# Beacon attention and low-rank mixer on one core: the first pair's masks ahead of casts, and three turns by DMA kept apart from the loads

## The chip, the cores and the metric

The kernel runs on one core of one Trainium2 chip. The core has a matmul engine (TensorE, "PE" in the profile; its weight loads are "PEld"), a vector engine (VectorE, "DVE"), a scalar engine (ScalarE, "ACT"), a general engine (GpSimd, "POOL") and a sync engine (SyncE, "SP"). Each works through its own instructions in order and waits on semaphores of the others. In this kernel POOL issues nearly all loads, and SP issues the first loads, all transposes by DMA and all stores. The metric is device time in microseconds (us), the median of several runs; lower is better.

## The reference

Batch 8, 8 heads, 576 tokens, 16 beacon tokens, head size 64. The attention's output, heads side by side, is the input of a mixer with a low-rank mixing over tokens and an MLP over channels.

```python
k_all = concat([beacon_k, k], axis=2);  v_all = concat([beacon_v, v], axis=2)
scores = (q @ k_all.T) / sqrt(64)
scores[:, 16:] is masked causally; the 16 beacons are seen by all
a = softmax(scores);  x = (a @ v_all), heads merged: (8, 576, 512)
h = (x.transpose(0, 2, 1) @ U) @ V          # rank 32, over the 576 tokens
u = x + h.transpose(0, 2, 1)
out = u + relu(u @ w_ch1) @ w_ch2           # 512 -> 2048 -> 512
```

## The kernel before

**Pairs.** Heads are treated two at a time: 8 batches of 4 pairs, pairs 0 to 31, so batch 4 is pairs 16 to 19. For one pair the work is as follows. Its q and its k are *grouped*: a copy puts the main 512 tokens of the two heads into a pair tile `pr` (`regroup`, L245 to L247). Then q and k are *transposed*, so that the head size lies on the partitions. For early pairs TensorE does that (`qkT_units`, L249; `tps`). For the others a DMA on SP does it (`turn_pair`, L274 to L280, `raw<-pr`), and a copy from `raw` puts the tokens in order (`order_units`, L282). The tokens that are left over, and the beacons, are turned for all pairs of a batch at once, ahead of the batch's first turn (`turn_heads`, L266, `qT<-hd`, `kT<-hd`). The scores come in two visits of TensorE (`visit`, L304, `sps`), each followed by four exponentials on ACT (L317) into one of four tiles `expt`. Masking is a minimum with a constant on DVE, after the exponentials (`mask_head`, L296: L298 and L300, twice for a pair). Then TensorE multiplies with v (`av_unit`, L331, `po`); a column of ones in v gives the sum, and DVE multiplies with its reciprocal into `xb` (L343, L344).

**Mixing and MLP.** When a batch's four pairs are done, `mix_units` (L359) gives u. From batch 3 on the mixing reads the attention's output turned by DMA (`turn_x`, L352, `xt<-xb`); `mlp_units` (L416) turns u back for the last sum (`ut<-uT`, L425). A block of the MLP is 512 rows: 16 units that compute `gps` (L435, with an eviction by ACT or DVE, L439 and L441) and 16 that compute `cps` (L452, L465). These units wait in a queue.

**Order by hand.** The order on each engine is the order of the words of `SCRIPT` (L687), which `step` (L634) carries out one by one; each engine gets its own instructions in that order, with no scheduler behind it. A number n takes n units from the MLP's queue. `Gk16` with an engine's letter in between, as in `GkA16`, groups k of pair 16 on ACT (V: DVE, G: POOL); `TqV17` is the copy, or the transposes and their copies, that leaves q of pair 17 ready; `R16` issues pair 16's turn on SP, with the batch's head turns if it is the first; `Sa16` and `Sb16` are the two visits of scores with their exponentials (`:2` puts two dummy matmuls ahead, which keep TensorE at work, and `I1` is one such dummy alone); `M16` masks; `A16.0` and `A16.1` multiply with v; `X3.0` to `X3.2` mix batch 3; `x12` turns a part of it; `k5`, `q5`, `v4`, `b5` issue the loads of batch 5's k and q, of batch 4's v and of batch 5's beacon keys on POOL; `Z16` is a copy of one element of pair 16's turned tile on POOL, which makes POOL wait until the turn has landed. In the kernel before, no `Z` stands in the script.

**Buffers.** Pair tiles and `raw` tiles have three buffers each, the load tiles two, `expt` is four tiles (two pairs), and v has two tiles, for even and odd batches. All PSUM tiles come from one pool of eight banks.

The places that the change touches are two: the first microseconds, in which pairs 0 to 3 are cast, scored and masked (their q and k come as 32-bit numbers and are cast while they are grouped), and the stretch in which batch 3 is computed and batch 4's first pairs are turned. There, in the kernel before, the script has: turn 15, then the loads `v4`, then (behind pair 16's grouping on ACT) turn 16; turn 17, then the loads `k5` and `q5`; turn 18 further on.

Of the kernel before, what the change touches and what calls it, by code (L numbers as in the profile page):

```python
# [27 lines left out]
def kernel(  # L28
# [605 lines left out]
    def step(t):  # L634
# [51 lines left out]

    SCRIPT = """  # L687
        v0A u GqA0 I8 GqG1 b1 GkV0 I2 GkG2 HqA0 TqA0 s B 1 v0B HkV0 TkV0 Sa0:3 GkV1 I3 1 TqV1 Sb0 1 TkV1 GqV2
        q1A Sb1 I1 GkV3 M0 GqV3 TkA2 1 w10 cG Sa1:2 TqV2 k1A A0.1 TqV3 M1 TkV3 A0.0 Sb2 Sa2:1 A1.1 A1.0 M2 w11
        q1B Sa3:1 w13 A2.0 GqV5 1 GkG5 Sb3 A2.1 w12 M3 TqA5 eA GqA4 GkA4 I2 A3.0 A3.1 X0.0 X0.1 X0.2 v1A TqA4  # L690
        w20 TkV5 k1B TkA4 w21 3 v1B 1 GqV6 Sb5 1 GqA7 Sa4 1 q2 2 Sb4 2 M4 4 A4.0 Sa5:0 2 GkA6 GkV7 M5 1 TqV6 1
        A5.1 TkA6 b3 A5.0 k2 1 A4.1 TkA7 Sa6:0 1 Sb6 TqV7 GqV8 2 GqV9 Sa7 2 M6 Sb7 b2 1 v2 A6.1 GkV9 GkV8 M7 1
        TqV8 2 GkV10 1 A6.0 GqA10 TqA10 q3 1 A7.1 A7.0 2 X1.0 X1.1 X1.2 TkA10 TqV9 TkV9 1 TkA8 1 Sa9 Sa8 3 Sb8
        1 k3 GqA11 1 v3 Sb9 M8 2 A8.1 A8.0 1 GkV12 1 GqV12 Sa10 1 M9 GkV11 R12 Sb10 1 M10 1 TkV11 1 A10.0
        TqA11 4 GkA13 A9.1 A9.0 Sa11 1 TkV12 GqV15 Sb11 1 k4 A10.1 2 GkA14 GqV13 1 TqA12 b5 Sa12 1 GqA14 M11
        R13 R14 3 GkA15 Sb12 1 A11.0 1 TkV13 M12 A11.1 q4 b4 TqA13 Sa13 R15 A12.0 TkA14 TqV14 1 TqV15 1 GkA16
        GqA16 1 R16 2 Sb13 v4 1 A12.1 M13 X2.0 2 Sb14 GkA17 A13.0 X2.1 TkV15 X2.2 A13.1 Sa14 GqA17 R17 Sb15 k5
        q5 GqA18 1 M14 1 Sa15 x12 3 TkV16 A14.1 TqA16 1 A14.0 k6 4 M15 GkA18 x13 1 R18 TkA17 1 TqV17 Sb16 2
        Sa16 A15.1 GkA19 M16 2 A15.0 TqA18 2 GqA19 x14 GkV20 x15 1 GkA21 1 R19 Sa17 1 A16.0 Sb17 2 GqV20 A16.1
        1 M17 TkA18 Sb18 X3.0 2 X3.1 1 Sa18 A17.0 1 GqA21 M18 1 X3.2 1 TkA19 R20 1 R21 1 GkV22 b6 1 TqA19  # L700
        A18.0 A18.1 v5 1 A17.1 Sa19 4 x18 1 Sb19 TqV20 TkV20 2 M19 GqA22 1 x16 R22 Sb20 A19.1 q6 Sa20 3 M20 1
        TkA21 x17 1 A19.0 1 TqA21 1 A20.0 TqV22 v6 1 GkV23 GqA23 1 x19 R23 Sa21 TkV22 X4.0 1 k7 1 Sb21 1 M21 1
        X4.1 1 A20.1 Sa22 1 A21.0 1 GkV25 GqV24 1 TqA23 GkV24 1 b7 R24 1 TkV23 Sb22 1 q7 A21.1 x20 X4.2 1
        GqA26 M22 GqV25 4 Sa23 x21 A22.0 TkA24 1 Sb23 R25 1 M23 2 A22.1 1 TqA24 A23.1 GkA26 1 R26 Sa24 2 A23.0
        2 Sb24 x22 2 TkA25 TqA25 v7 5 GqV27 1 M24 GkV27 Sa25 2 x23 TkV26 1 A24.0 R27 1 Sb25 TqV26 M25 X5.0
        A24.1 GqV28 2 Sb26 1 GkA28 R28 A25.0 2 x24 Sa26 TqV27 1 X5.1 4 X5.2 1 GkV30 1 TkA27 M26 1 TkV28 A25.1
        GkV29 Sa27 GqV29 2 Sb27 1 A26.0 x25 1 R29 1 M27 A26.1 TqV28 GqA30 1 R30 A27.1 GkV31 2 Sa28 A27.0 1 x26
        1 TqV29 Sb28 2 M28 2 GqV31 TqA30 1 TkA29 TkA30 Sa29 1 X6.0 R31 Sb29 A28.1 x27 A28.0 4 TkV31 2 TqV31 1
        M29 1 Sa30 1 A29.0 2 x28 X6.1 2 Sb30 A29.1 X6.2 4 x29 Sa31 M30 10 Sb31 A30.0 A30.1 2 x30 M31 4 A31.0
        A31.1 2 X7.0 4 x31 1 X7.1 3 X7.2 2  # L710
    """

    with tc.manual_schedule(engines={ENG.PE, ENG.Activation, ENG.DVE, ENG.SP, ENG.Pool}):
# [118 lines left out]
```

## Time and profile before

| | |
|---|---|
| median of 3 runs | 359.29 us (359.05 to 359.36) |
| the profiled execution | 361.73 us, its span 360.1 us |
| TensorE busy | 347.2 us, 96% of the span |
| ACT, DVE, POOL busy | 205.2, 189.9, 84.0 us |
| data moved by DMA | 43.57 MB |

The page gives busy time by engine, the busy tenths in 40 slices, the DMA queues, the chain of work that ended last, the costliest groups, and the DMA issues with the time from issue to landing. In the order of time, a row has its start, its length, the engine, the line, the operation, what it writes and reads, how many instructions are merged in it, and in brackets the engine's idle time before it with the work that ended that wait. A row in which several instructions are merged can hold small gaps.

### The profile page before, as it was taken

Reading aid. Unit: us, or ns where it says so; the run is one execution under the profiler, and the core shown is the slowest. Engines: PE = TensorE matmul, PEld = TensorE weight load, DVE = VectorE, ACT = ScalarE, POOL = GpSimd, SP = SyncE. Lnnn points to the kernel's source line nnn. Section 1 sums busy time; section 2 is a strip of 40 time slices with the busy share of each in tenths; the row PEclk is TensorE's granted clock in tenths of the full one; section 3 lists DMA queues with packets and bytes.
Section 4 is the critical chain, followed back from the end, with each engine's and each line's share of the span. In section 5 each row is a group of like instructions: output and inputs, shape, how many; then the busy total and the mean of one; then the engine's idle time right before and its main releaser. Section 6 shows DMA issues by size and latency. Waiting matters only on the chain.

```text
span 360.1 us, 7694 instructions
## 1 busy us (share of the span) xinstructions
PE 347.2 (96%) x3022; PEld 177.2 (49%) x3022; DVE 189.9 (53%) x530; ACT 205.2 (57%) x432; POOL 84.0 (23%) x123
## 2 busy tenths in 40 slices
PE   7789999999999989999999999999999999999995
PEld 3455478844545435454444444454544544444444
DVE  3775355546649454574767427675554447313311
ACT  4885867399579868658653963678335302401300
POOL 7966648601308005400630050000000000000000
PEclk9989999999999999999999999999999999999998
DMA  9999999992959999996899694563333123013112
GB/s 191 174 172 187 183 191 164 202 160 40 164 127 129 117 162 111 175 223 106 94 163 194 139 107 107 111 116 61 88 100 66 20 76 103 16 58 90 31 48 76
DMA packets 134396, 43.57 MB, mean 121 GB/s; under 512 B 106545, under 2 KB 130353, under 8 KB 134353
## 3 DMA queue, kind: packets, MB, share of 16 engines
q0 software_dynamic: 69008, 17.54, 51.8%
q1 hardware_dynamic: 64752, 25.14, 34.9%
q8 instruction: 25, 0.41, 0.5%
q10 hardware_dynamic: 592, 0.34, 0.3%
q14 instruction: 19, 0.15, 0.1%
HBM read 37.63 MB, written 9.44 MB: 131 GB/s over the span
## 4 chain that ended last, share of the span: by engine, by line
PE 86%; DMA 6%; DVE 2%; ACT 2%; SPq 1%; issue 1%
PE cps L452 35%; PE gps L435 32%; PE po L335 8%; PE sps L311 7%; DMA raw<-pr 4%; DMA sth<-in_q_dram 2%; ACT expt L317 1%; DMA stm<-in_q_dram 1%; PE tps L257 1%; PE ups L394 1%; PE ups L401 1%; PE qtp L375 1%; SPq L190 1%; DVE xb L344 1%; SPq L184 1%
## 5 line engine op out<-in xcount | busy, mean ns | idle before, releaser
L317 ACT ACTIVATE expt<-sps 128x496 f16<-128x496 f32 (+2 forms) x256 | 111.6, 544 | 43.2 <-PE sps L311 39.2
L452 PE MATMUL cps<-w,gT 128*128 128x512 f16 (+1 forms) x656 | 134.2, 353 | 0.0
L435 PE MATMUL gps<-uT,w 128*128 128x512 f16 x576 | 132.7, 379 | 1.1 <-DVE xb L344 1.1
L439 ACT ACTIVATE gT<-gps 128x512 f16<-128x512 f32 x86 | 52.2, 625 | 70.4 <-PE gps L435 70.2
L452 PEld LDWEIGHTS <-gT 128*128 128x128 f16 x656 | 60.5, 98 | 57.5 <-issue 4.4
L435 PEld LDWEIGHTS <-w 128*128 128x128 f16 x576 | 53.0, 98 | 65.1 <-issue 3.5
L441 DVE TENSOR_SCALAR gT<-gps 128x512 f16<-128x512 f32 x58 | 40.0, 690 | 49.5 <-PE gps L435 48.6
L465 DVE TENSOR_TENSOR ob<-cps,ut 128x512 f32<-128x512 f32 (+1 forms) x33 | 22.2, 674 | 47.0 <-PE cps L452 46.6
L335 PEld LDWEIGHTS <-expt 128*128 128x128 f16 (+1 forms) x960 | 36.0, 99 | 14.5 <-DVE expt L298 4.0
L197 POOL DMA_DIRECT2D vs<-in_v_dram x50 | 40.0, 811 | 7.2 <-DMA st<-in_k_dram 4.0
L335 PE MATMUL po<-vs,expt 128*128 128x65 f16 (+1 forms) x960 | 39.2, 195 | 2.3 <-ACT expt L317 1.4
L311 PE MATMUL sps<-qT,kT 64*128 64x80 f16 (+4 forms) x384 | 35.7, 282 | 2.1 <-ACT expt L317 1.2
L344 DVE TENSOR_TENSOR xb<-po,rec 128x320 f16<-128x320 f32 x64 | 31.5, 492 | 2.2
L298 DVE TENSOR_TENSOR expt<-expt,bigmask 128x512 f16<-128x512 f16 x64 | 26.7, 418 | 9.2 <-ACT expt L317 9.2
L343 DVE RECIPROCAL rec<-po 128x5 f32<-128x5 f32 x64 | 12.0, 188 | 28.0 <-PE po L335 27.2
L311 PEld LDWEIGHTS <-kT 64*128 64x128 f16 x384 | 12.5, 94 | 24.4 <-issue 16.4
L187 POOL DMA_DIRECT2D vs<-in_beacon_v_dram x10 | 5.4, 540 | 68.1 <-PE po L335 68.0
L408 DVE TENSOR_TENSOR uT<-ups,xt 128x240 f16<-128x240 f32 (+3 forms) x40 | 15.6, 450 | 7.2 <-PE ups L401 7.2
L518 ACT ACTIVATE pr<-st 128x512 f16<-128x512 f16 x26 | 16.8, 658 | 0.8 <-DMA st<-in_k_dram 0.8
L190 POOL DMA_DIRECT2D st<-in_k_dram x8 | 6.8, 856 | 40.7 <-ACT gT L439 22.9
L518 ACT ACTIVATE qT<-raw 128x512 f16<-128x512 f16 x10 | 11.1, 1105 | 5.3 <-DMA raw<-pr 5.3
L300 DVE TENSOR_TENSOR expt<-expt,mask 80x80 f16<-80x80 f16 x64 | 12.2, 191 | 0.0
(78 smaller groups left out, 170.7 us busy)
## 6 DMA issues: line engine op xcount, KB each, us to landing
out_dram<-ob SPq DMA_DIRECT2D x31, 256.0 KB, 2.2
st<-in_q_dram POOLq DMA_DIRECT2D x6, 512.0 KB, 9.8
st<-in_k_dram POOLq DMA_DIRECT2D x6, 512.0 KB, 8.4
vs<-in_v_dram POOLq DMA_DIRECT2D x18, 128.0 KB, 6.7
w<-in_moe_w_ch_dram POOLq DMA_DIRECT2D x4, 512.0 KB, 8.8
w<-in_moe_w_ch_dram POOLq DMA_DIRECT2D x2, 1024.0 KB, 12.1
out_dram<-ob SPq DMA_DIRECT2D x10, 128.0 KB, 5.7
stm<-in_k_dram SPq DMA_DIRECT2D x4, 256.0 KB, 4.6
```

The lines of the kernel that those rows point to most:

```text
L197: nc.gpsimd.dma_start(out=dst[a : a + nq[j], j, :, :], in_=src[hs, ds(q0[j], nq[j]), :].rearrange("h p d -> p h d"))
L298: nc.vector.tensor_tensor(out=e4, in0=e4, in1=bigmask, op=ALU.min)
L311: nc.tensor.matmul(ps[g, i][:, ds(o, w)], kT[hp, c, ds(P * ch, P)], qT[hp, c, ds(qa, w)], start=True, stop=True,)
L317: nc.scalar.activation(out=ex[i][:, ds(PAD + SLOT * g, gw[g])], in_=ps[g, i][:, 0 : gw[g]], func=AF.Exp, scale=scale)
L335: nc.tensor.matmul(po[:, j, :], ex[0 : nk[c], ds(blk[(c, j)], P)], vs[0 : nk[c], ds(c * H * E + h * E, E)], start=(c == 0), stop=(c == j),)
L344: nc.vector.tensor_tensor(out=xb[:, h // 2, :, ds(D * (h % 2), D)], in0=po[:, :, 0:D], in1=r.broadcast_to([P, NT, D]), op=ALU.mult)
L435: nc.tensor.matmul(g[:, 0:n], w1[:, cc, ts(dc, P)], uT[:, cc, ds(ring(t0), n)], start=(cc == 0), stop=(cc == NCC - 1))
L439: nc.scalar.activation(out=gT["t"][:, dc, 0:n], in_=g[:, 0:n], func=AF.Relu)
L441: nc.vector.tensor_scalar_max(out=gT["t"][:, dc, 0:n], in0=g[:, 0:n], scalar1=0.0)
L452: nc.tensor.matmul(ps[:m, :], gT["t"][:, dc, ds(P * i, m)], w2[:, dc, ds(cs, w)], start=(dc == 0), stop=turned and dc == NDC - 1, skip_gro ...
L465: nc.vector.tensor_tensor(out=ob[:m, :], in0=ps[:m, :], in1=gT["u"][:m, i, ds(cs, w)], op=ALU.add)
L518: nc.scalar.activation(out=out, in_=in_, func=AF.Copy)
```

## The change

Only the script changes. In the first stretch: `M0` (pair 0's masks) moves ahead of `GkV3` (the cast of pair 3's k); `TqV2` moves from behind `Sa1` to ahead of `GqV3`; `A0.0` moves up to stand right behind `A0.1`. In the second stretch: pair 16 is grouped on DVE and not on ACT, right behind turn 15, and its turn `R16` follows; `Z16` is put ahead of the loads `v4`; pair 18 is grouped right behind turn 17 (q on ACT as before, k on DVE and not on ACT) and its turn `R18` follows; `Z18` is put ahead of the loads `k5` and `q5`. The number of MLP units between `TqV15` and `Sb13` stays four. The remaining words keep their order; the script's later lines are only wrapped otherwise.

```diff
-        q1A Sb1 I1 GkV3 M0 GqV3 TkA2 1 w10 cG Sa1:2 TqV2 k1A A0.1 TqV3 M1 TkV3 A0.0 Sb2 Sa2:1 A1.1 A1.0 M2 w11
+        q1A Sb1 I1 M0 TkA2 GkV3 TqV2 GqV3 1 w10 cG Sa1:2 k1A A0.1 A0.0 TqV3 M1 TkV3 Sb2 Sa2:1 A1.1 A1.0 M2 w11
...
-        R13 R14 3 GkA15 Sb12 1 A11.0 1 TkV13 M12 A11.1 q4 b4 TqA13 Sa13 R15 A12.0 TkA14 TqV14 1 TqV15 1 GkA16
-        GqA16 1 R16 2 Sb13 v4 1 A12.1 M13 X2.0 2 Sb14 GkA17 A13.0 X2.1 TkV15 X2.2 A13.1 Sa14 GqA17 R17 Sb15 k5
-        q5 GqA18 1 M14 1 Sa15 x12 3 TkV16 A14.1 TqA16 1 A14.0 k6 4 M15 GkA18 x13 1 R18 TkA17 1 TqV17 Sb16 2
...
+        R13 R14 3 GkA15 Sb12 1 A11.0 1 TkV13 M12 A11.1 q4 b4 TqA13 Sa13 R15 GkV16 GqV16 R16 A12.0 TkA14 TqV14
+        1 TqV15 4 Sb13 Z16 v4 1 A12.1 M13 X2.0 2 Sb14 GkA17 A13.0 X2.1 TkV15 X2.2 A13.1 Sa14 GqA17 R17 GqA18
+        GkV18 R18 Sb15 Z18 k5 q5 1 M14 1 Sa15 x12 3 TkV16 A14.1 TqA16 1 A14.0 k6 4 M15 x13 1 TkA17 1 TqV17
+        Sb16 2 Sa16 A15.1 GkA19 M16 2 A15.0 TqA18 2 GqA19 x14 GkV20 x15 1 GkA21 1 R19 Sa17 1 A16.0 Sb17 2
```

More of the change, by code (lines that the diff above doesn't have):

```diff
@@ L695 @@
         TqA11 4 GkA13 A9.1 A9.0 Sa11 1 TkV12 GqV15 Sb11 1 k4 A10.1 2 GkA14 GqV13 1 TqA12 b5 Sa12 1 GqA14 M11
-        R13 R14 3 GkA15 Sb12 1 A11.0 1 TkV13 M12 A11.1 q4 b4 TqA13 Sa13 R15 A12.0 TkA14 TqV14 1 TqV15 1 GkA16
-        GqA16 1 R16 2 Sb13 v4 1 A12.1 M13 X2.0 2 Sb14 GkA17 A13.0 X2.1 TkV15 X2.2 A13.1 Sa14 GqA17 R17 Sb15 k5
-        q5 GqA18 1 M14 1 Sa15 x12 3 TkV16 A14.1 TqA16 1 A14.0 k6 4 M15 GkA18 x13 1 R18 TkA17 1 TqV17 Sb16 2
-        Sa16 A15.1 GkA19 M16 2 A15.0 TqA18 2 GqA19 x14 GkV20 x15 1 GkA21 1 R19 Sa17 1 A16.0 Sb17 2 GqV20 A16.1
@@ L700 @@
[L700 to L709, printed above, removed]
@@ L710 @@
-        A31.1 2 X7.0 4 x31 1 X7.1 3 X7.2 2
+        R13 R14 3 GkA15 Sb12 1 A11.0 1 TkV13 M12 A11.1 q4 b4 TqA13 Sa13 R15 GkV16 GqV16 R16 A12.0 TkA14 TqV14
+        1 TqV15 4 Sb13 Z16 v4 1 A12.1 M13 X2.0 2 Sb14 GkA17 A13.0 X2.1 TkV15 X2.2 A13.1 Sa14 GqA17 R17 GqA18
+        GkV18 R18 Sb15 Z18 k5 q5 1 M14 1 Sa15 x12 3 TkV16 A14.1 TqA16 1 A14.0 k6 4 M15 x13 1 TkA17 1 TqV17
+        Sb16 2 Sa16 A15.1 GkA19 M16 2 A15.0 TqA18 2 GqA19 x14 GkV20 x15 1 GkA21 1 R19 Sa17 1 A16.0 Sb17 2
+        GqV20 A16.1 1 M17 TkA18 Sb18 X3.0 2 X3.1 1 Sa18 A17.0 1 GqA21 M18 1 X3.2 1 TkA19 R20 1 R21 1 GkV22 b6
@@ new lines @@
+        1 TqA19 A18.0 A18.1 v5 1 A17.1 Sa19 4 x18 1 Sb19 TqV20 TkV20 2 M19 GqA22 1 x16 R22 Sb20 A19.1 q6 Sa20
+        3 M20 1 TkA21 x17 1 A19.0 1 TqA21 1 A20.0 TqV22 v6 1 GkV23 GqA23 1 x19 R23 Sa21 TkV22 X4.0 1 k7 1 Sb21
+        1 M21 1 X4.1 1 A20.1 Sa22 1 A21.0 1 GkV25 GqV24 1 TqA23 GkV24 1 b7 R24 1 TkV23 Sb22 1 q7 A21.1 x20
+        X4.2 1 GqA26 M22 GqV25 4 Sa23 x21 A22.0 TkA24 1 Sb23 R25 1 M23 2 A22.1 1 TqA24 A23.1 GkA26 1 R26 Sa24
+        2 A23.0 2 Sb24 x22 2 TkA25 TqA25 v7 5 GqV27 1 M24 GkV27 Sa25 2 x23 TkV26 1 A24.0 R27 1 Sb25 TqV26 M25
@@ L711 @@
+        X5.0 A24.1 GqV28 2 Sb26 1 GkA28 R28 A25.0 2 x24 Sa26 TqV27 1 X5.1 4 X5.2 1 GkV30 1 TkA27 M26 1 TkV28
+        A25.1 GkV29 Sa27 GqV29 2 Sb27 1 A26.0 x25 1 R29 1 M27 A26.1 TqV28 GqA30 1 R30 A27.1 GkV31 2 Sa28 A27.0
+        1 x26 1 TqV29 Sb28 2 M28 2 GqV31 TqA30 1 TkA29 TkA30 Sa29 1 X6.0 R31 Sb29 A28.1 x27 A28.0 4 TkV31 2
+        TqV31 1 M29 1 Sa30 1 A29.0 2 x28 X6.1 2 Sb30 A29.1 X6.2 4 x29 Sa31 M30 10 Sb31 A30.0 A30.1 2 x30 M31 4
+        A31.0 A31.1 2 X7.0 4 x31 1 X7.1 3 X7.2 2
     """
```

## The prediction

> **What bounds the kernel now.** I read the page first, then the busy time by stretches, then the chain of work and the order of time in the two places that the change touches.
>
> ```profile
> PE 347.2 (96%) x3022; PEld 177.2 (49%) x3022; DVE 189.9 (53%) x530; ACT 205.2 (57%) x432; POOL 84.0 (23%) x123
> ...
> PE cps L452 35%; PE gps L435 32%; PE po L335 8%; PE sps L311 7%; DMA raw<-pr 4%; DMA sth<-in_q_dram 2%; ACT expt L317 1%; DMA stm<-in_q_dram 1%; PE tps L257 1%; PE ups L394 1%; PE ups L401 1%; PE qtp L375 1%; SPq L190 1%; DVE xb L344 1%; SPq L184 1%
> ```
>
> TensorE is busy 96% of the span and carries 86% of the chain. What the change can win is TensorE's gaps, and there is one large entry on the chain that isn't an engine: the turn of a pair, `raw<-pr`, 4%.
>
> ```profile
> 110.00:115.00 5.00, 4.47 (x79) 2.73 (x78) 4.47 (x12) 5.00 (x12) 5.00 (x7) 1.00 1.53 108
> ...
> 125.00:130.00 5.00, 4.49 (x26) 1.87 (x22) 0.79 (x2) 0.82 (x1) 0.00 (x0) 1.00 1.27 151
> 130.00:135.00 5.00, 4.19 (x23) 1.54 (x24) 4.40 (x11) 5.00 (x11) 0.00 (x0) 1.00 1.22 154
> ```
>
> The columns are the stretch, its length, then busy PE, PEld, DVE, ACT, POOL, clock, DMA. Outside the first 30 us, TensorE idles mainly here: 0.5 us in 110 to 115 and 1.3 us in 125 to 135, where DVE and ACT stop together. The chain and the order of time say why:
>
> ```profile
> 116.10 13.06 DMA raw<-pr
> ```
>
> ```profile
> 129.18 1.18 ACT L518 ACTIVATE qT<-raw 128x512 f16<-128x512 f16 x1 [4.62 <-DMA raw<-pr]
> 129.19 0.70 DVE L285 COPY kT<-raw 128x512 f16<-128x512 f16 x1 [5.06 <-DMA raw<-pr]
> ...
> 130.56 1.04 PE L435 MATMUL gps<-uT,w 128*128 128x512 f16 x4 [1.07 <-DVE xb L344]
> ...
> 133.89 1.57 PE L311 MATMUL sps<-qT,kT 64*128 64x496 f16 x4
> ...
> 141.78 0.58 PE L311 MATMUL sps<-qT,kT 64*128 64x496 f16 x4
> ```
>
> Pair 16's turn takes 13.06 us. TkV16 (DVE) and TqA16 (ACT) wait for it; the evictions queued behind them stop, the eight banks fill, and TensorE loses 1.07 us, then another 0.99 (a score visit of 1.57 where a free one takes 0.58): 2.06 us. What stands ahead of the turn:
>
> ```profile
> 109.09 4.19 POOL L197 DMA_DIRECT2D vs<-in_v_dram  x5
> 113.25 0.91 POOL L190 DMA_DIRECT2D st<-in_k_dram  x1
> ...
> 114.80 0.92 POOL L190 DMA_DIRECT2D st<-in_q_dram  x1
> ...
> 116.10 8.31 SPq L277 DMA_TRANSPOSE raw<-pr  x2
> ```
>
> ```profile
> DMA to landing us min/median/max: 3.1/3.3/13.1
> ```
>
> ```profile
> vs<-in_v_dram POOLq DMA_DIRECT2D x3, 128.0 KB, 4.6
> ...
> st<-in_k_dram POOLq DMA_DIRECT2D x1, 512.0 KB, 10.8
> ...
> st<-in_q_dram POOLq DMA_DIRECT2D x1, 512.0 KB, 15.6
> ...
> raw<-pr SPq DMA_TRANSPOSE x2, 12.6
> ...
> st<-in_k_dram POOLq DMA_DIRECT2D x1, 512.0 KB, 6.1
> ```
>
> Batch 4's v and batch 5's k and q are issued from 108.6 to 116.4, just ahead of turns 16 and 17, which land after 12.6 us on average where the median turn takes 3.3. The last row is batch 4's k, loaded at 88.93 with nothing beside it: 6.1 us; batch 5's k among the turns took 10.8.
>
> **The change, part by part.** *Turn 16.* Its casts go from ACT to DVE, right after A11.1, and the turn with its two head turns follows turn 15 on SP, ahead of an output's store. Batch 4's v, at 108.6 to 109.1 in the rows above, is released by A11.1's matmuls, so DVE comes to the casts within a microsecond of that, and two of 0.28 to 0.48 us (rows below) are through by 111. So turn 16 is issued near 111, with no load in flight, and lands near 114.3 with the median. Its copies come to their turn at 124.1 (129.19 less the wait of 5.06): both waits are gone. I book all of the 2.06 us; bounds -2.1 and 0 (the wait reappears, see the rivals).
>
> *Z16 and Z18* are one-element copies on POOL that wait for turns 16 and 18. Behind them POOL holds only loads. v moves from 108.6 to about 114.6, is issued by 119.3 and, at the 4.6 us of its row, is in near 124; it is wanted by A16.0, a step that stands behind GkV20 (139.78, below). Nothing.
>
> *Turns 17 and 18.* Turn 17 is issued when its ACT cast is done, near 120 as before, but now only v is ahead. With v in by 124 I put turn 17's landing at 125.5 and turn 18's at 126.5. TkA17 stands behind five MLP units, 20 matmuls that TensorE does up to the gap before 130.56, so ACT comes to it near 129. Batch 5's k is then issued at 126.7 and lands, between 6.1 and 10.8 us, at 132.8 to 137.5.
>
> ```profile
> 139.78 0.48 DVE L247 COPY pr<-st 128x512 f16<-128x512 f16 x1
> ...
> 141.88 0.69 DVE L465 TENSOR_TENSOR ob<-cps,ut 128x512 f32<-128x512 f32 x1 [1.61 <-PE cps L452]
> ...
> 144.46 0.28 DVE L247 COPY pr<-st 128x512 f16<-128x512 f16 x1
> ```
>
> The first reader is GkV20 at 139.78, so at 137.7 once 2.1 us are won, with 1.61 us of slack behind it on DVE; q's is the copy at 144.46 (then 142.4), and q, issued 1.6 us after k, lands within 136 to 144. Covered, narrowly: zero. The xt and ut turns on SP stand behind turn 18 now; the ut turn is first read at 141.88, some 10 us later. Zero.
>
> *The casts that moved.* ACT loses GkA16 and GqA16 and DVE gains two of 0.28 to 0.48 us. ACT's GqA18 now stands before pair 15's exponentials, not behind them, and GkV18 is one more on DVE near 118, where it waits over a microsecond for TensorE.
>
> ```profile
> 111.63 1.17 ACT L518 ACTIVATE pr<-st 128x512 f16<-128x512 f16 x2
> ...
> 114.03 0.62 PE L335 MATMUL po<-vs,expt 128*128 128x65 f16 x15 [0.23 <-ACT expt L317]
> ...
> 121.05 0.69 ACT L518 ACTIVATE pr<-st 128x512 f16<-128x512 f16 x1
> ```
>
> From 110 to 115 ACT is full (5.00) and TensorE waits 0.53 us: best case that all goes, -0.5. But DVE is 4.47 busy there, and 0.56 to 0.96 more makes it the late one for M13: worst case +0.5. I take +0.1. GqA18 keeps the banks of pair 15's scores 0.69 us longer; TensorE's next visit may wait for them: 0 to +0.7, I take +0.3, since ACT must also now do in 11 us what it did without a pause from 129.18.
>
> *The start.* M0 moves ahead of GkV3, TqV2 ahead of GqV3; A0.0 comes right behind A0.1, and TensorE turns pair 2's q before pair 1's scores.
>
> ```profile
> 12.85 0.62 DVE L247 CAST pr<-stm 128x512 f16<-128x512 f32 x1 [0.36 <-DMA stm<-in_k_dram]
> ...
> 13.52 0.41 DVE L298 TENSOR_TENSOR expt<-expt,bigmask 128x512 f16<-128x512 f16 x1
> ...
> 15.23 0.22 DVE L574 CAST hd<-sth 80x128 f16<-80x128 f32 x1 [0.27 <-DMA sth<-in_q_dram]
> ...
> 17.07 6.87 ACT L317 ACTIVATE expt<-sps 128x496 f16<-128x496 f32 x16 [1.22 <-issue]
> ...
> 19.30 0.49 DVE L344 TENSOR_TENSOR xb<-po,rec 128x320 f16<-128x320 f32 x1
> ...
> 21.43 0.62 PE L335 MATMUL po<-vs,expt 128*128 128x65 f16 x15 [1.21 <-ACT expt L317]
> ```
>
> M0 (four instructions from 13.52, two of them of 0.41 us) starts where DVE waits 0.36 us for pair 3's k, and the 0.27 us for its q heads falls behind TqV2: 0.63 us of DVE waits at best. The next limit is the run of 16 exponentials from 17.07: its first scores now stand behind pair 3's two turns on TensorE, which need the cast at 15.23, and can come some 0.4 us sooner. Against that, A0.0 (0.49 us and its reciprocal) ahead of M1 delays pair 1, +0.3 if no wait is saved. Bounds -0.6 and +0.3; I take -0.4, ACT's end.
>
> **The sum:** -2.06 + 0.1 + 0.3 - 0.4 = -2.1. The profiled execution took 361.73 us (span 360.1 and 1.6 around it), so 359.6; the median of the runs, 359.29, is 2.4 below that execution, and -2.1 makes it 357.2. Later on TensorE has hardly a gap (0.4 of 180 us idle), so what is won should last:
>
> ```profile
> 140.00:320.00 180.00, 179.63 (x1460) 84.59 (x1459) 99.36 (x258) 97.61 (x192) 21.05 (x28) 1.00 0.69 107
> ```
>
>  Its bounds add to -3.2 and -0.6 with the turn won: 356.1 to 358.7.
>
> **The rivals.** *The clock.* TensorE runs at half clock once after the start:
>
> ```profile
> 23.00:24.00 1.00, 0.69 (x9) 0.35 (x6) 0.96 (x4) 1.00 (x4) 0.20 (x1) 0.79 1.36 151
> 24.00:25.00 1.00, 1.00 (x4) 0.28 (x3) 0.83 (x4) 1.00 (x4) 0.00 (x0) 0.50 1.19 152
> ...
> 26.00:27.00 1.00, 1.00 (x23) 0.91 (x21) 0.69 (x2) 0.47 (x1) 0.33 (x1) 0.51 1.28 199
> ...
> 25.19 1.86 PE L335 MATMUL po<-vs,expt 128*128 128x65 f16 x30
> ```
>
> ```profile
> 157.62 1.08 PE L335 MATMUL po<-vs,expt 128*128 128x65 f16 x30
> ```
>
> Thirty small matmuls took 1.86 us where they take 1.08 at full clock, 0.78 more, on the way to the first mixing; with the two dummies before them I put the half-clock stretch at 1.2 us, an estimate. It follows the gaps at 20 to 23.4 us, which the change moves. If it vanishes: 357.2 - 1.2 = 356.0; if a second one arises: 358.4.
>
> The Trainium skill (TensorE: Matmul & The Clock Gate, "Part 1: The HAM clock gate") says that the clock is halved by a free-running window of about 3.4 us of low activity; the trace agrees, its half clock beginning in the slice at 23 (0.79) and still there in the one at 26 (0.51). By that rule a shift of a few tenths can decide whether the window trips; no row here shows where the limit lies.
>
> *The wait moves to turn 17.* If turn 17 took 12.6 us again it would land at 132.5, 3.5 us after ACT wants it. The 5.06 us of before cost 2.06 on TensorE, 0.41 each, so this costs 1.4 to 1.6: 358.8. For it: v is still in flight. Against: then v, k and q stood around it, 1.18 MB each by their shapes, now v alone.
>
> The Trainium skill (DMA: Bandwidth & Descriptors, "Issuing engines are not separate DMA queues") says that transfers of all issuing engines share the same 16 engines and interleave. The trace agrees (12.6 against 3.3 us); by it turn 17 still pays for v, and not for k and q.
>
> *The other side: the held loads are late.* k hangs on turn 18. Should turn 18 take 12.6 us from 121.3, it lands at 133.9, k (10.8 us) at 144.8, 7.1 us after GkV20; at 0.41 that is 2.9 us: 357.2 + 2.9 = 360.1, and q behind it can only add. It decides once k comes 5 us late, so when turn 18 lands after 132. Against: again only v is ahead.
>
> **Chances.** The forecast 0.58; no half clock 0.11; a second one 0.07; turn 17 late 0.10; loads late 0.14. A change under 0.2% (0.7 us) is about what a measurement of this kernel can't tell from none. Faster: 0.56 of the forecast, 0.11, 0.04 and 0.04 of the next two, 0.75; same: the rest of these, 0.11; slower 0.14. The range, 355.9 to 359.7, leaves out the late loads and some of the vanished half clock.
>
> **What the changed profile would show.** Right: turn 16 landing in 3 to 5 us near 115; no wait of DVE or ACT on `raw` near 129; the gap of 1.07 gone; batch 5's k issued near 127; the first of the 16 exponentials near 16.7. Wrong: POOL's wait for a turn of over 8 us, `DVE pr <- DMA st` in the list of waits, or a longer stretch at half clock.

## The result and the profile after

| | before | after |
|---|---|---|
| median | 359.36 us (358.56 to 360.78, 7 runs) | 357.67 us (356.92 to 358.16, 7 runs) |
| ratio of the times | | 0.9944, 95% interval 0.9926 to 0.9963 |
| the profiled execution | 361.73 us, span 360.1 | 357.11 us, span 355.4 |

The changed kernel is faster by 0.56%; of 359.36 us that is 2.0 us, between 1.3 and 2.7 (the two medians by themselves lie 1.7 us apart). The two profiled executions differ by 4.6 us, so more than two of these come from something else, which the first views below settle. First the page of the changed kernel, its span, busy times and chain:

```profile
span 355.4 us, 7696 instructions
...
PE 345.0 (97%) x3022; PEld 176.1 (50%) x3022; DVE 189.8 (53%) x533; ACT 203.6 (57%) x429; POOL 84.3 (24%) x125
...
PE 79%; DVE 2%; ACT 1%; issue 0%
PE cps L452 33%; PE gps L435 31%; PE po L335 7%; PE sps L311 6%; PE ups L401 1%; PE qtp L375 1%; PE ups L394 1%; ACT expt L317 1%; PE tps L257 1%; DVE xb L344 0%; DVE qT L285 0%; ACT qT L518 0%; ACT pr L518 0%; DVE ob L465 0%; DVE expt L298 0%
```

This chain could be followed back to 57.79 us only, so its shares don't compare with those of before. But 116 us, where `raw<-pr` had 4% of the chain before, lies within it, and `raw<-pr` is gone. Where the time went is read best from marks that both kernels pass: the first matmuls of the MLP (`gps`) and of each batch's mixing (`qtp`). TensorE's rows in order of time, before:

```profile
30.74 1.03 PE L435 MATMUL gps<-uT,w 128*128 128x512 f16 x4
...
112.20 0.46 PE L375 MATMUL qtp<-xb,Usb 128*32 128x128 f16 x20
147.69 0.47 PE L375 MATMUL qtp<-xb,Usb 128*32 128x128 f16 x20
...
290.67 0.47 PE L375 MATMUL qtp<-xb,Usb 128*32 128x128 f16 x20
```

and after:

```profile
28.14 3.62 PE L435 MATMUL gps<-uT,w 128*128 128x512 f16 x16
...
110.21 0.47 PE L375 MATMUL qtp<-xb,Usb 128*32 128x128 f16 x20
143.02 0.46 PE L375 MATMUL qtp<-xb,Usb 128*32 128x128 f16 x20
...
286.01 0.47 PE L375 MATMUL qtp<-xb,Usb 128*32 128x128 f16 x20
```

At batch 2's mixing the changed kernel is 1.99 us ahead; between the mixing of batch 2 and that of batch 3, 35.49 us have become 32.81, another 2.68; from there to batch 7's mixing both take the same (142.98 and 142.99). So nothing is given back later. Most of the first 1.99 us is the half clock of the profile before, which this execution doesn't have; the middle experiment below, whose start is that of the kernel before, shows it.

The stretches of the changed kernel (columns as in the prediction):

```profile
110.00:115.00 5.00, 4.53 (x105) 3.36 (x102) 4.93 (x16) 4.80 (x14) 2.63 (x5) 1.00 0.51 102
...
125.00:130.00 5.00, 5.00 (x30) 2.22 (x29) 3.15 (x8) 3.71 (x8) 2.19 (x3) 1.00 1.06 125
130.00:135.00 5.00, 5.00 (x52) 2.51 (x50) 3.44 (x11) 4.78 (x11) 0.85 (x1) 1.00 1.48 173
```

TensorE's holes in 125 to 135 (4.49 and 4.19 busy before) are closed; the small one in 110 to 115 (4.47, now 4.53) is as it was. And the order of time in the changed kernel:

```profile
108.51 1.88 SPq L277 DMA_TRANSPOSE raw<-pr  x1
...
112.03 0.18 POOL L665 COPY gate<-raw 1x1 f16<-1x1 f16 x1 [20.90 <-DMA raw<-pr]
...
117.19 4.21 SPq L277 DMA_TRANSPOSE raw<-pr  x2
121.68 1.24 ACT L518 ACTIVATE qT<-raw 128x512 f16<-128x512 f16 x1
121.90 0.61 DVE L285 COPY kT<-raw 128x512 f16<-128x512 f16 x1
122.87 5.34 PE L435 MATMUL gps<-uT,w 128*128 128x512 f16 x24
123.51 0.18 POOL L665 COPY gate<-raw 1x1 f16<-1x1 f16 x1 [6.25 <-DMA raw<-pr]
124.02 0.88 POOL L190 DMA_DIRECT2D st<-in_k_dram  x1 [0.34 <-issue]
...
130.38 0.58 PE L311 MATMUL sps<-qT,kT 64*128 64x496 f16 x4
...
134.64 0.47 DVE L247 COPY pr<-st 128x512 f16<-128x512 f16 x1
```

Turn 16 is issued at 108.51 and has landed at 112.03. (The 20.90 in brackets is all of POOL's idle time ahead of `Z16`, not the turn's time; before, POOL had stood idle for 15.44 us when it came to v at 108.58.) Its copies, at 121.68 and 121.90, wait for nothing: 24 matmuls run in one row where the wait of 1.07 us was, and the score visit takes 0.58 us. The time from issue to landing of turn 16, of turns 17 and 18, and of batch 5's k and q:

```profile
raw<-pr SPq DMA_TRANSPOSE x1, 3.5
...
raw<-pr SPq DMA_TRANSPOSE x2, 5.0
...
st<-in_k_dram POOLq DMA_DIRECT2D x1, 512.0 KB, 7.2
...
st<-in_q_dram POOLq DMA_DIRECT2D x1, 512.0 KB, 10.1
```

### The profile page after: what moved, and what is told of

It is laid out like the page before. It is cut to its first block, busy times and chain, and to the rows that moved or that the text cites. A ratio compares the mean times of both kernels' runs of the same rounds, so it can differ in the third digit from the quotient of the medians.

```text
span 355.4 us, 7696 instructions
## 1 busy us (share of the span) xinstructions
PE 345.0 (97%) x3022; PEld 176.1 (50%) x3022; DVE 189.8 (53%) x533; ACT 203.6 (57%) x429; POOL 84.3 (24%) x125
## 4 chain that ended last, share of the span: by engine, by line
PE 79%; DVE 2%; ACT 1%; issue 0%
PE cps L452 33%; PE gps L435 31%; PE po L335 7%; PE sps L311 6%; PE ups L401 1%; PE qtp L375 1%; PE ups L394 1%; ACT expt L317 1%; PE tps L257 1%; DVE xb L344 0%; DVE qT L285 0%; ACT qT L518 0%; ACT pr L518 0%; DVE ob L465 0%; DVE expt L298 0%
## 5 line engine op out<-in xcount | busy, mean ns | idle before, releaser
L335 PEld LDWEIGHTS <-expt 128*128 128x128 f16 (+1 forms) x960 | 34.9, 98 | 13.8 <-DVE expt L298 3.3
L335 PE MATMUL po<-vs,expt 128*128 128x65 f16 (+1 forms) x960 | 38.3, 194 | 1.6 <-DVE expt L298 1.5
L311 PE MATMUL sps<-qT,kT 64*128 64x80 f16 (+4 forms) x384 | 34.9, 282 | 1.5 <-DVE kT L259 1.1
L518 ACT ACTIVATE pr<-st 128x512 f16<-128x512 f16 x23 | 14.8, 661 | 1.9 <-DMA st<-in_k_dram 1.8
L247 DVE COPY pr<-st 128x512 f16<-128x512 f16 x32 | 9.9, 327 | 3.5 <-DMA st<-in_q_dram 3.1
```

The source lines that it names most:

```text
L311: nc.tensor.matmul(ps[g, i][:, ds(o, w)], kT[hp, c, ds(P * ch, P)], qT[hp, c, ds(qa, w)], start=True, stop=True,)
L335: nc.tensor.matmul(po[:, j, :], ex[0 : nk[c], ds(blk[(c, j)], P)], vs[0 : nk[c], ds(c * H * E + h * E, E)], start=(c == 0), stop=(c == j),)
```

## The experiments

Theories. A: the gain is turn 16's earlier issue, and nothing else matters. B: the holds (`Z16`, `Z18`) are needed, since they keep the later turns free of k and q. C: the start carries a part. Each run was measured in turn with the kernel before on its chip; the first four shared one chip (before: 359.8 us, 29 runs), the last four another (360.1 us, 23 runs).

| kernel | median (range, runs) | ratio to before (95%) |
|---|---|---|
| start alone | 360.17 (358.86 to 362.21, 12) | 1.0019 (0.9994 to 1.0045) |
| middle alone | 357.60 (357.24 to 358.18, 11) | 0.9943 (0.9922 to 0.9964) |
| turns, no hold | 357.69 (357.46 to 358.85, 11) | 0.9943 (0.9919 to 0.9967) |
| holds alone | 364.69 (363.94 to 365.92, 5) | 1.0144 (1.0106 to 1.0182) |
| turn 16 alone | 357.28 (356.95 to 357.90, 6) | 0.9935 (0.9911 to 0.9960) |
| casts on ACT | 358.08 (357.49 to 359.37, 12) | 0.9957 (0.9939 to 0.9975) |
| hold of v alone | 363.51 (362.34 to 364.28, 6) | 1.0113 (1.0088 to 1.0138) |
| both holds, turn 18 early | 358.02 (357.63 to 359.94, 12) | 0.9959 (0.9941 to 0.9977) |

### The start and the middle, each by itself

The start alone is the kernel before with the change's first hunk; the middle alone is the changed kernel with this hunk taken back:

```diff
-        q1A Sb1 I1 GkV3 M0 GqV3 TkA2 1 w10 cG Sa1:2 TqV2 k1A A0.1 TqV3 M1 TkV3 A0.0 Sb2 Sa2:1 A1.1 A1.0 M2 w11
+        q1A Sb1 I1 M0 TkA2 GkV3 TqV2 GqV3 1 w10 cG Sa1:2 k1A A0.1 A0.0 TqV3 M1 TkV3 Sb2 Sa2:1 A1.1 A1.0 M2 w11
```

> The kernel before with the change of the first stretch alone (M0 ahead of GkV3, TqV2 ahead of GqV3, A0.0 behind A0.1); pair 16's and pair 18's grouping, the turns and the loads as before, no Z. Theory T (most of the gain is the turn of pair 16 that no longer lands behind the loads; the start gives about 0.4 us): -0.4 us on the median, between 0 and -0.8, with the wait of DVE and ACT for raw near 129 still 4 to 5 us. Rival S (the start carries the gain, since both profiles show the first MLP matmul 2.6 us apart at 30 us): -1.5 to -2 us. Rival C (the half-clock stretch at 24 us of the profile before is in most runs of before, and the change removes it): as S, with a clock under 0.995 in the profile of before and 1.0 here.

> The changed kernel with the first stretch put back: only the turns of pairs 16 to 18 in a row, their casts on DVE where the change has them, and the loads held by Z16 and Z18. Theory T: -1.3 us or more on the median (357.2 to 358.0 if before is 359.3), turn 16 landing in 3 to 5 us, no wait for raw on DVE or ACT, TensorE without the gap of 1.07. Rival S: within 0.5 us of before, although the wait is gone.

The middle alone has the whole gain, the start alone none: theory C falls. The -0.4 that was expected of the start alone isn't there, nor rival S's -1.5; the waits on `raw` near 129 us are, 4.06 us on ACT and 4.50 on DVE, as expected. Rival C falls too: the half clock is absent from the start alone's profile (mean granted clock 1.000, before 0.993) and the time is no better; and of the 52 runs of the kernel before on the two chips nine have a clock of 0.995 or less, not most.

The profiles say how a start that does run earlier can come to nothing. Three rows of DVE in order of time: the copy of batch 2's q, near 56 us, in the middle alone,

```profile
55.50 0.29 DVE L247 COPY pr<-st 128x512 f16<-128x512 f16 x1 [1.79 <-DMA st<-in_q_dram]
```

in the changed kernel,

```profile
56.21 0.29 DVE L247 COPY pr<-st 128x512 f16<-128x512 f16 x1 [3.10 <-DMA st<-in_q_dram]
```

and in the start alone:

```profile
56.40 0.29 DVE L247 COPY pr<-st 128x512 f16<-128x512 f16 x1 [3.27 <-DMA st<-in_q_dram]
```

The load sets this copy, and in the two kernels with the new start DVE waits longer for it (3.10 and 3.27 us against 1.79). At the first MLP matmul the changed kernel is 0.77 us ahead of the middle alone (28.14 against the row below); at batch 2's mixing, 110.21 against 110.36, 0.15 are left. The middle alone, TensorE's rows in order of time:

```profile
28.91 2.32 PE L435 MATMUL gps<-uT,w 128*128 128x512 f16 x10
...
110.36 0.47 PE L375 MATMUL qtp<-xb,Usb 128*32 128x128 f16 x20
143.18 0.47 PE L375 MATMUL qtp<-xb,Usb 128*32 128x128 f16 x20
```

One pair of executions is thin evidence, for the same start doesn't always arrive at the same time. Of the eight profiles with the old start, six have the full clock all through 7 to 31 us: they reach the first MLP matmul at 28.24 to 28.92 us, the two with the new start at 28.14 and 28.19. At batch 2's mixing it is 109.70 to 110.66 against 110.21 and 110.40, so nothing is left. The loss lies ahead of batch 1's mixing: from the first MLP matmul to there the new start takes 39.16 and 39.30 us, those six 38.55 to 38.83; from there to batch 2's mixing all take 42.9. That DVE's wait near 56 us is the cause is argued, not shown by a run of its own. What speaks for it: in the eight kernels with the old start, too, that stretch is longer than 38.55 us by 0.78 where DVE waits 3.20 us at this copy (turns without holds), by 0.28 at 2.94 (the holds alone), and by at most 0.21 at 2.52 or less.

The rows also price the half clock. The middle alone has the start of the kernel before, but it came to its MLP at 28.91 and not 30.74: 1.83 us less, in an execution without a half clock there (all six: 1.8 to 2.5 us less). So the profile of before had a half clock that the same start doesn't always have, and about 1.8 us of the gap of 4.6 between the two profiled executions is that.

### Turn 16 alone

The kernel before with nothing but pair 16's grouping and turn moved (to DVE and behind turn 15):

```diff
-        ... A11.1 q4 b4 TqA13 Sa13 R15 A12.0 TkA14 TqV14 1 TqV15 1 GkA16 GqA16 1 R16 2 Sb13 v4 ...
+        ... A11.1 q4 b4 TqA13 Sa13 R15 GkV16 GqV16 R16 A12.0 TkA14 TqV14 1 TqV15 4 Sb13 v4 ...
```

> The kernel before with one thing changed: pair 16 is grouped on DVE right behind turn 15 and turned there. Turns 17 and 18, their casts and all loads as before, no copy that holds a load. Theory E, from the run without holds (only when turn 16 is issued counts): the whole gain of the middle, 2.0 us on the median, within 0.5; turn 16 lands in 5 to 7 us, turn 17 in 8 to 10, TensorE without the gap of 1.07. Rival R (the three turns in a row, or the casts of pair 18 moved off ACT, carry part): half the gain or less, with a wait of ACT for raw of over 2 us at turn 17.

It has the whole gain, 2.3 us (1.4 to 3.2), as theory A has it; rival R, by which the other turns or casts carry half of it, falls. Its order of time:

```profile
108.86 2.16 SPq L277 DMA_TRANSPOSE raw<-pr  x1
...
111.83 0.89 POOL L190 DMA_DIRECT2D st<-in_k_dram  x1
...
117.79 1.24 SPq L277 DMA_TRANSPOSE raw<-pr  x1
...
122.28 1.23 ACT L518 ACTIVATE qT<-raw 128x512 f16<-128x512 f16 x1
...
127.64 1.19 ACT L518 ACTIVATE kT<-raw 128x512 f16<-128x512 f16 x1
```

Here nothing is held: turn 16 goes out while v is being issued and takes 7.4 us, turn 17 goes out 6 us behind k and takes 8.7. Both are slower than in the changed kernel (3.5, 5.0), and neither is waited for. The stretch from batch 2's mixing to batch 3's takes 32.57 us (110.56 to 143.13), about as in the changed kernel (32.81).

### The holds taken away, and the holds alone

Turns without holds is the middle alone less the two `Z`. The holds alone are the kernel before with a `Z16` ahead of v and a `Z17` ahead of k and q, and all turns where they were; in the third kernel only v is held:

```diff
-        ... 4 Sb13 Z16 v4 1 ... R18 Sb15 Z18 k5 q5 ...
+        ... 4 Sb13 v4 1 ... R18 Sb15 k5 q5 ...
...
-        ... R16 2 Sb13 v4 1 ... R17 Sb15 k5 q5 ...
+        ... R16 2 Sb13 Z16 v4 1 ... R17 Sb15 Z17 k5 q5 ...
...
-        ... R16 2 Sb13 v4 1 ...
+        ... R16 2 Sb13 Z16 v4 1 ...
```

> As the middle alone, but without the two copies Z16 and Z18: turns early, loads free to start as before. Theory T (what counts is what stands ahead of a turn in the DMA engines): turn 16 is issued near 111 behind batch 4's v and lands in 5 to 9 us, in time; turns 17 and 18 stand behind batch 5's k and q and land in 10 to 13 us, so ACT waits for turn 17 by 2 to 4 us and the gain is 0.4 to 1.2 us smaller than with the holds. Rival E (issuing turn 16 earlier is all): the same as the middle alone within 0.3 us.

> The kernel before with two one-element copies on POOL added and nothing moved: one that waits for turn 16 ahead of batch 4's v, one that waits for turn 17 ahead of batch 5's k and q. Turns and casts where they were. Theory T: turn 16, issued near 116 as before, lands in 3 to 5 us near 120, the waits for raw near 129 go, and the gain is that of the middle alone within 0.5 us; batch 5's k is issued near 127. Rival E (the early issue is what counts): no gain, or a loss, since turn 16 is issued as late as before.

> The kernel before with one copy added: batch 4's v waits on POOL for turn 16; batch 5's k and q follow v on POOL without a copy of their own; no turn moves. Theory H (a held load becomes a load that stands ahead of a later turn): turn 16 lands in 3 to 4 us near 117 and turn 17 in 5 to 8, but k and q are issued from 121 to 125 and turn 18, issued near 128 where it always was, lands in 9 to 13 us; ACT waits 3 to 7 us for it, and the time is 1 to 4 us above before. Rival: the loads are through by turn 18, and the gain is that of the middle.

Without the holds the ratio is the same, 0.9943, and not 0.4 to 1.2 us worse as theory T expected; turns 17 and 18 then take 8.3 us on average and not 10 to 13. Turn 17, issued at 118.72, lands near 127, and ACT wants it at 128.54, so it is just in time. So theory B falls: in this change the holds buy no time that can be measured.

By themselves the holds cost 4 to 5 us, where theory T expected the whole gain from the two of them. Yet they do to turn 16 just what they are for: it lands in 3.1 us in both kernels. The hold of v alone, which came out much as theory H expected, in order of time:

```profile
120.96 0.92 POOL L190 DMA_DIRECT2D st<-in_k_dram  x1
...
129.59 4.06 SPq L277 DMA_TRANSPOSE raw<-pr  x1
...
139.87 1.07 ACT L518 ACTIVATE qT<-raw 128x512 f16<-128x512 f16 x1 [6.29 <-DMA raw<-pr]
...
142.49 0.77 PE L311 MATMUL sps<-qT,kT 64*128 64x208 f16 x2 [3.41 <-ACT expt L317]
```

POOL issues in order, so what is held for turn 16 comes out all the later: k and q, issued before at 113.25 and 114.80, now at 120.96 and 122.50. There they stand ahead of the next turn, 18, issued at 129.59, and ACT waits 6.29 us for it. The slow turn has moved by two pairs and costs more, because ACT's exponentials stand behind it. With both holds the same happens (turn 18 issued 128.38, 12.6 us, ACT waits 6.46). After the stall comes a half clock on top; TensorE's row at the end of the stall, and the stretches, of the holds alone:

```profile
143.61 0.78 PE L311 MATMUL sps<-qT,kT 64*128 64x208 f16 x2 [3.58 <-ACT expt L317]
```

```profile
140.00:145.00 5.00, 1.30 (x6) 0.38 (x4) 0.67 (x2) 4.01 (x8) 1.81 (x2) 0.83 1.42 176
145.00:150.00 5.00, 5.00 (x26) 2.18 (x24) 0.69 (x2) 2.29 (x5) 2.33 (x3) 0.50 1.77 182
```

TensorE stood idle for 3.58 us, and then worked at half clock all through 145 to 150. The Trainium skill (TensorE: Matmul & The Clock Gate, "Part 1: The HAM clock gate") says that the clock falls to half after an idle window of about 3.4 us; these rows agree, with TensorE idle from 140.03 to 143.61 and the fall at 143.34. A window that is idle throughout isn't needed for it, as the last section shows.

### The hold mended

If turn 18 behind the held loads is the cost, moving turn 18 ahead of them must cure it. This is the kernel before with both holds of the change, `Z16` ahead of v and `Z18` ahead of k and q; pair 16 is where it was before, and pair 18's grouping (k on DVE) and turn are moved as in the change:

```diff
-        ... Sb13 v4 1 ... GqA17 R17 Sb15 k5 q5 GqA18 1 M14 ... M15 GkA18 x13 1 R18 TkA17 ...
+        ... Sb13 Z16 v4 1 ... GqA17 R17 GqA18 GkV18 R18 Sb15 Z18 k5 q5 1 M14 ... M15 x13 1 TkA17 ...
```

> The kernel before with both holds (v behind turn 16, batch 5's k and q behind turn 18) and with pair 18's casts and turn moved up behind turn 17, as in the change; pair 16's casts stay on ACT and its turn stays where it was. Theory H: the loss of the holds alone (5 us) is gone because no turn stands behind the held k and q; turn 16 is issued near 114 and lands in 3 to 4 us; the time is that of the middle alone within 0.5 us. Rival: the holds cost by themselves (k and q too late for pair 20's casts), and the time stays above before.

It does: 0.9959, from 1.0113 with the hold of v alone and 1.0144 with both holds and turn 18 left behind. DVE's copies of batch 5's k and q in this kernel, in order of time:

```profile
136.28 0.30 DVE L247 COPY pr<-st 128x512 f16<-128x512 f16 x1 [0.89 <-DMA st<-in_k_dram]
...
141.92 0.29 DVE L247 COPY pr<-st 128x512 f16<-128x512 f16 x1 [1.39 <-DMA st<-in_q_dram]
```

k is issued at 127.95 here, 3.9 us later than in the changed kernel, and now DVE does wait for it, 0.89 and 1.39 us; the ratio shows no loss by it that stands out of its interval. So there are two cures for the slow turn 16, and one is enough: issue it ahead of the loads, or hold the loads for it and for every turn that would then come behind them.

### The casts' engine

The middle alone with pair 16's casts, in their new place, on ACT as before:

```diff
-        ... R15 GkV16 GqV16 R16 ...
+        ... R15 GkA16 GqA16 R16 ...
```

> The middle alone, with pair 16's two casts on ACT and not on DVE, at the same early place. ACT was full from 110 to 115, so if the cast's engine matters: turn 16 is issued 1 to 2 us later than with DVE, still ahead of everything that it waited behind, and TensorE's idle time in 105 to 118 grows by 0.3 to 1 us; the median is 0.3 to 1 us above the middle alone. If the engine doesn't matter: the same within 0.3 us.

0.9957 against 0.9943 on DVE, on two chips, with intervals that overlap by more than half: by the times, whether DVE is the better engine for them isn't settled. Turn 16 is issued at 109.61, 0.95 us later than in the middle alone, and TensorE is busy for 12.34 us of 105 to 118 against 12.40, so the 0.3 to 1 us of idle time that was expected isn't seen. But the stretch from batch 2's mixing to batch 3's takes 33.49 us, and 33.46 in the kernel of "The hold mended", whose casts of pair 16 are on ACT as well; the four kernels that have them on DVE and no stall take 32.57 to 33.07. That points to 0.4 to 0.9 us for the engine, from one execution of each.

What the two kernels with these casts on ACT do settle is that the wait by itself is worth most of the gain: without it they are 1.5 us faster than before (0.9 to 2.2, and 0.8 to 2.1), with no work of pair 16 taken off ACT (pair 18's k cast is on DVE in both).

## Why the prediction was right

The forecast was 357.2 us, measured are 357.67. The sum of -2.1 stands against -2.0 (-2.7 to -1.3). By its steps:

| step of the prediction | forecast | measured |
|---|---|---|
| turn 16's wait | -2.06 | turn 16 alone: -2.3 (-3.2 to -1.4), its casts on DVE included; with them on ACT: -1.5 (-2.2 to -0.9) |
| Z16, Z18, turns 17 and 18 | 0 | with and without the holds 0.9943 |
| casts moved, GqA18 early | +0.1, +0.3 | not seen: the middle alone -2.1 (-2.8 to -1.3), no worse than turn 16 alone by more than the intervals; pair 16's casts on DVE perhaps -0.4 to -0.9 |
| the start | -0.4 | the start alone +0.7 (-0.2 to +1.6) |

*Turn 16* was right in place, and in size as far as the runs can tell: the 2.06 lies inside all the intervals, but with the casts left on ACT the best value is 1.5. It is issued 2.5 us sooner than the 111 of the prediction, of which 2 us are only that all of this execution is that much ahead by then. "No wait on `raw` near 129" holds, and the gap of 1.07 is gone.

*Turns 17 and 18* land in 5.0 us on average, k is issued at 124.02 (forecast 126.7), and its first reader at 134.64 doesn't wait. Of the signs of being wrong, neither is one here: POOL's 20.90 and 6.25 us ahead of the two `Z` are idle time, with turns of 3.5 and 4.6 us in them, and the one `DVE pr <- DMA st` on the page's list is mostly the copy near 56 us. The rivals "the wait moves to turn 17" and "the held loads are late" did not occur in this execution; in that of the middle alone DVE did wait 1.19 us for the held q, and its time is no worse. Turn 16 alone shows by how much the first was off: even unheld, 8.7 us was soon enough. The second was a better guess than its form in the prediction: a hold can cost 4 us here, but by way of a turn behind the held k and q, and the change's early turn 18 shuts that way. The prediction booked the move of turn 18 at nothing; without it, a hold would have made the kernel slower.

*The start* is the step that failed. Its first part was right: the first of the 16 exponentials begins at 16.19 us (forecast 16.7; 16.87 in the middle alone, 16.45 to 17.09 in the six executions with the old start and a full clock). But the step put this into the sum as time won at the end. The prediction had looked for idle time of TensorE from 140 us on only, and not between 30 and 110 us; the lead is gone by batch 1's mixing at 67 us, and the row near 56 us is the likely place.

*The casts*, +0.4 together, show nowhere as a loss; for pair 16's the profiles point to a gain, which would be nearer to the step's best case (-0.5) than to the +0.1 that it took.

*The half clock* as a rival ("if it vanishes: 356.0") was a wrong kind of rival. It is absent from the changed kernel's profile, but at that place also from the seven other profiles with the old start, so the change didn't decide it. It was priced at 1.2 us; the first MLP matmuls with the same start give 1.8. The medians, which average over it, are the ones to compare.

So the mechanism was right where most of the gain is, and the closeness of the total is in part luck: the -0.4 of the start that did not last and the +0.4 of the casts that is not seen cancelled.

## What to carry to other kernels

A small transfer that an engine waits for is best issued ahead of the bulk loads, even by an earlier cast on whatever engine is free; how early is read from the moment of the loads' issue, not from the moment at which it is wanted. A load that is held back for one such transfer must be followed to the next one, for it comes out later and stands ahead of that. And a gain at the start is worth nothing until it has been followed past every later wait for a load: one row with `<-DMA` in brackets may take it back.

## What the runs showed of the hardware

Turns by DMA that are issued behind batch 5's k and q land about when q does. Issue and landing (issue plus the time to landing), all in us:

| kernel, turn | q issued | q lands | turn issued | turn lands |
|---|---|---|---|---|
| before, turn 16 | 114.80 | 130.4 | 116.10 | 129.2 |
| before, turn 17 | 114.80 | 130.4 | 119.83 | 132.0 |
| start alone, turn 16 | 112.99 | 128.6 | 114.10 | 126.8 |
| start alone, turn 17 | 112.99 | 128.6 | 118.03 | 130.0 |
| turns without holds, turn 17 | 114.29 | 125.6 | 118.72 | 127.3 |
| turns without holds, turn 18 | 114.29 | 125.6 | 120.08 | 128.1 |
| turn 16 alone, turn 17 | 113.38 | 124.8 | 117.79 | 126.5 |
| hold of v alone, turn 18 | 122.50 | 137.8 | 129.59 | 139.9 |
| holds alone, turn 18 | 125.97 | 139.7 | 128.38 | 141.0 |

That is from 1.8 us ahead of q to 2.5 behind it, though the turns come from another engine's queue and that of the hold of v alone is issued 7 us after q. With no load ahead turn 16 takes 3.1 to 4.0 us in six kernels. The Trainium skill (DMA: Bandwidth & Descriptors, "Issuing engines are not separate DMA queues") says that transfers of all engines run on the same 16 engines and interleave. That the engines are shared, these rows bear out; a small transfer that interleaved evenly with a larger one would be expected to pass it clearly, and no row here shows more than 1.8 us of that. How the engines share between the two queues packet by packet, the runs don't tell.

Between 7 us and the end of its work, TensorE's half clock comes in whole pieces of 3.41 us: 23.57 to 26.98 in the profile of before, 11.98 to 15.40 in turns without holds, 142.53 to 145.94 in the hold of v alone, and two in a row, 143.34 to 150.17, in the holds alone. In the 3.41 us just ahead of the fall TensorE was busy for 1.89, 1.78, 0.04 and 0.10 us. So the stretch need not be idle: somewhat over half busy was still too little. Busy time alone doesn't set the limit, though: counted on from the changes of the clock, the pieces 349.83 to 353.25 of the middle alone, with 1.71 busy us, and 7.96 to 11.37 of casts on ACT, with 1.99, were not followed by a fall. What else counts, the runs don't tell. Coming back takes more: after 3.04 busy us at half clock it stayed at half (the holds alone), after 3.29 it rose (the hold of v alone). That the half clock depends on where the pieces fall on TensorE's gaps would explain how one start can have it in one execution and not in the next; no run was made to show it.

The late turn may also make a kernel's time vary. After, the middle alone, turns without holds, turn 16 alone and casts on ACT, in which turn 16 goes out early, span 0.9 to 1.9 us from lowest to highest in 6 to 12 runs; the start alone, with the late turn, over 3.4 us in 12 runs, and the kernel before over 3.2 and 3.9 us in 23 and 29. Against it stands the kernel of "The hold mended", without a late turn and over 2.3 us in 12 runs. That the traffic of the loads meets a late turn differently from run to run would explain a wider spread, but no run here was made to show that.
